# Attention on one core: a half product that waits for its partner by a semaphore of TensorE's own, and another order of the products of one step

## The chip, the cores and the metric

The kernel runs on one core of a Trainium2 chip. The metric is the device time of the whole program in microseconds (us): the median of 3 runs, beside one further execution that the hardware profiler recorded.

## The reference

Two transformer layers with shared weights, on 2048 rows of 640 numbers in float32. Each layer normalises its rows, runs an attention block with 32 heads of 20 numbers, adds the result to the rows, normalises again and runs a dense block with a squared ReLU. The part that matters here is the attention:

```python
scores = jnp.einsum("bhqd,bhkd->bhqk", q, k) * (Dh ** -0.5)
p = _softmax(scores, axis=-1)
o = jnp.einsum("bhqk,bhkd->bhqd", p, v)
```

The softmax needs the largest score of every query, so the kernel computes the scores twice: once with the queries on the partitions, to take the maximum along a row, and once with the keys on the partitions, with the maximum already subtracted, for the exponential.

## The kernel before

Heads are taken in groups of four and queries in blocks of 512: 8 groups by 4 blocks are 32 blocks of work (`NBLK`) in a layer. In a block the 2048 keys are passed in 16 steps of 128 (`NKT`). Per layer there are thus 512 steps. A head has 20 numbers, kept three times for a product in split precision, so a product contracts 60 (or 62, with the maximum) rows. Two such products fit TensorE's 128 rows side by side: `par` 0 uses rows 0 to 63, `par` 1 uses rows 64 to 127. Below they are called the lower and the upper rows.

An attention step has four kinds of work, named by letters in a hand-written order (`ORDERS`, read by `op`), which sets the order of the instructions on every engine:

- `a`, `b`: a score product (line 596), keys on the partitions, 512 queries wide, on the lower rows (`a`) or the upper ones (`b`), into one of four PSUM banks in turn. ScalarE (ACT) takes the exponential of each (line 603), which frees the bank.
- `m`, `n`: a whole product for the maxima (line 481, called from `smax`), queries on the partitions, 512 keys wide, on the lower (`m`) or upper (`n`) rows. VectorE (DVE) reduces it to a maximum (line 493), which frees the bank.
- `u`, `w`: a product for the maxima over half of the keys (256 wide, line 481, called from `smax_half`), first on the lower rows (`u`), then on the upper ones (`w`), into the two halves of one bank. One reduction on DVE (line 521) takes both.
- `V`: the exponentials times the values (line 608), eight matmul instructions on all rows, into the accumulator of the block (bank 7). It takes the exponentials of the step before.

The products for the maxima share banks 4, 5 and 6 in turn. Twelve pairs of such products are due in eight steps, whose order is `"mbubanawV" * 8`; nearly all steps of both layers use it. As the steps run ahead, the maxima belong to later blocks.

The matmuls of `u` and `w` write to one bank from two halves of the rows, so `w` is kept back until `u` is done. Before the change this goes over DVE: an empty instruction (`mark`) in DVE's queue waits for `u`, and `w` waits for that. Once a block, ACT also copies the accumulator out of PSUM (line 621).

Of the kernel before, what the change touches and what calls it, by code (L numbers as in the profile page):

```python
# [39 lines left out]
def tile_layers(  # L40
# [11 lines left out]
    nc = tc.nc  # L52
# [250 lines left out]
    def after(later, earlier, reason="one half of the rows adds to the bank that the other half has left"):  # L303
        tc.add_manual_dep(
            later.ins,
            earlier.ins.name,
            mybir.DependencyInfo(mybir.DependencyClass.Sync, mybir.DependencyReason.DATA),
            reason=reason,
        )
# [161 lines left out]
    def maxima(t):  # L471
        if t not in mx_t:
            mx_t[t] = small.tile([P, 4, 4, 6], F32, tag="mx", bufs=14, name=name("mx"))
            if t in PARTLY:
                nc.vector.memset(mx_t[t][:, :, :, :4], LEAST)
        return mx_t[t]

    def by_queries(dst, t, p, sub, c, par, keys=slice(0, QB)):

        b = 64 * par  # L480
        return nc.tensor.matmul(  # L481
            dst,
            q_t[t][b : b + 60, p, sub * P : (sub + 1) * P],
            k_t[t // NQB, c][b : b + 60, p, keys],
            start=True,
            stop=True,
        )
# [7 lines left out]
        )  # L495

    halved = {}

    def two_columns(t):

        if t not in halved:
            halved[t] = True
            nc.gpsimd.memset(maxima(t)[:, :, :, 4:], LEAST)

    def column(*x):

        halved[x] = halved.get(x, 3) + 1
        assert halved[x] < 6
        return halved[x]

    def smax_half(bank, t, p, sub, c, half, par, earlier=None):

        w = QB // 2
        dst = bank[:, par * w : (par + 1) * w]
        m = by_queries(dst, t, p, sub, c, par, slice(half * w, (half + 1) * w))
        if earlier is None:
            mark = nc.vector.nop()
            after(mark, m)
            return mark
        after(m, earlier, "matmuls on two halves of the rows write to one bank in turn")  # L520
        nc.vector.tensor_reduce(  # L521
            maxima(t)[:, p : p + 3 : 2, sub, c if not half else column(t, p, sub)],
            bank.rearrange("q (r k) -> q r k", r=2),
            axis=AX.X,
            op=ALU.max,
        )

    def step_one(t, p, sub, x, par):

        dst = ps_q("sm")  # L530
        res = xtile("rl")[:, :QB]
        by_queries(dst, t, p, sub, x, par)
        nc.scalar.activation(res, dst, AF.Relu)  # L533
        return res
# [180 lines left out]
    def qkv(first, x_src, rest, scores):  # L715
# [275 lines left out]
        15: "anbmnanbaabmbnammbnaVbmbmmbVmbananVanmbanVnambmbVanbmnaVnmbaanVmbbanmV",  # L991
        14: "mbbbanmbbmambmVanannaVmbnaaanVbmabnmVanbmbmbVnaanmbVmabmbanVbmannaVn",
        13: "baanmbVmbanambbnbmVanbmnaVnaabnmbVanbmaanVnmbbanaVmnbmabVabbmmnaVm",
        12: "mbubanawV" * 8,
    }

    def attention(first, x_src, first_rows):
# [95 lines left out]
        def op(o):  # L1093
# [17 lines left out]
            elif o == "u":  # L1111
                if parts or next_pair(parts):
                    x = parts.pop(0)
                    bank = turn.pop(0)
                    opened.append((bank, x, smax_half(banks[:, bank, :], *x, 0)))
            elif o == "w":
                if opened:
                    bank, x, mark = opened.pop()
                    smax_half(banks[:, bank, :], *x, 1, mark)
                    turn.append(bank)  # L1120
                    did(x[0])
            else:
                i = state["done"]
                if i >= last or i < last - NKT and min(st_n) < 2 * (i + 1):
                    return
                t, u = divmod(i, NKT)
                if u == 0:
                    state["acc"] = banks[:, 7, :]
                pv(state["acc"], t, u, es_of.pop(i))
                state["done"] += 1  # L1130
                if u == NKT - 1:
                    steps = finish(t, state["acc"])
                    split.update((i + j, f) for j, f in zip((4, 6, 7, 9, 11, 12), steps))
                t = rows["next"]
                if rows["at"] is not None:
                    if state["begun"] >= rows["at"]:
                        mrows_load(t)
                        rows.update(next=t + 1, at=None)
                elif t in over and t in q_t and state["begun"] >= (t - 2) * NKT + 2:
                    mrows_max(t)  # L1140
                    mrows(t)
                    rows["at"] = state["begun"] + 2
# [417 lines left out]
```

## Time and profile before

| what | value |
|---|---|
| median of 3 runs | 3538.99 us (3538.1 to 3539.18) |
| profiled execution | 3538.19 us |
| its span, first to last instruction | 3536.2 us |
| granted TensorE clock in it | 1.000 of full speed |
| busy share of PE, DVE, ACT | 100%, 77%, 75% |
| reductions of two halves (line 521), that is steps with a `u` and a `w` | 982 |

PE is TensorE's matmuls, PEld its weight loads, which run beside matmuls. A matmul of this kernel is one weight load and one matmul instruction, and a wait in front of it shows at the weight load. The ends of matmuls are modelled in the profile, and a PE that is busy 100% of the time isn't one at its peak: what holds a step up is read from starts, and from the idle time in brackets with the instruction that ended it.

### The profile page before, as it was taken

How to read it: one execution, taken by the hardware profiler on the slowest of the kernel's cores; microseconds unless marked ns; L12 is line 12 of the kernel's file. 1: busy time of each engine (PE TensorE's matmuls, PEld its weight loads, DVE VectorE, ACT ScalarE, POOL GpSimd, SP SyncE). 2: the span in 40 equal slices, each digit the busy share in tenths (PEclk: the TensorE clock that was granted, in tenths of full speed). 3: DMA queues.
4: the chain of work that ended last, by engine and by line, in shares of the span. 5: the costliest groups of instructions: out<-in, count | busy, mean ns of one | idle time of the engine just before them, and what ended most of it. 6: DMA issues, size and time to landing. Idle time of an engine off the chain costs nothing.

```text
span 3536.2 us, 70757 instructions
## 1 busy us (share of the span) xinstructions
PE 3521.2 (100%) x26542; PEld 2264.2 (64%) x26542; DVE 2731.2 (77%) x5023; ACT 2652.9 (75%) x5208; POOL 809.5 (23%) x927
## 2 busy tenths in 40 slices
PE   9999999999999999999999999999999999999999
PEld 7897444444444446999988964444444444479998
DVE  8878999999999993456567789999999999824443
ACT  3778999999999995122237789999999999932221
POOL 6531444221221111111153201221211211211110
PEclk9999999999999999999999999999999999999999
DMA  9776555323211136734477652232232111376231
GB/s 304 274 233 175 172 156 157 109 70 82 57 48 49 46 110 209 249 106 111 135 269 249 197 150 76 65 82 61 67 82 59 46 48 43 115 226 238 75 82 38
DMA packets 377413, 452.78 MB, mean 128 GB/s; under 512 B 176642, under 2 KB 223746, under 8 KB 377070
## 3 DMA queue, kind: packets, MB, share of 16 engines
q1 hardware_dynamic: 376254, 445.89, 41.6%
q8 instruction: 209, 3.42, 0.4%
q10 hardware_dynamic: 816, 2.36, 0.2%
q14 instruction: 134, 1.10, 0.1%
HBM read 273.83 MB, written 174.30 MB: 127 GB/s over the span
## 4 chain that ended last, share of the span: by engine, by line
PE 95%; DVE 2%; ACT 1%; DMA 1%; issue 1%; POOL 0%; SPq 0%; DVEq 0%; ACTq 0%
PE banks L608 29%; PE banks L481 22%; PE banks L293 13%; PE banks L596 11%; PE banks L1326 10%; PE banks L331 9%; DVE mx L493 1%; ACT e L603 1%; PE banks L1158 0%; DMA q<-d_qk 0%; ACT e L1165 0%; DVE bst L244 0%; DVE xnT L257 0%; DVE x L252 0%; DMA d_qk<-ev 0%
## 5 line engine op out<-in xcount | busy, mean ns | idle before, releaser
L603 ACT ACTIVATE e<-banks 128x512 f32<-128x512 f32 x3968 | 2034.7, 613 | 10.3 <-PE banks L596 2.2
L493 DVE TENSOR_REDUCE mx<-banks 128x1 f32<-128x512 f32 x2094 | 1346.5, 686 | 187.2 <-PE banks L596 126.6
L481 PE MATMUL banks<-k,q 60*128 60x512 f32 x4568 | 1347.7, 374 | 3.0 <-DVE v L377 1.7
L481 PEld LDWEIGHTS banks<-k,q 60*128 60x128 f32 x4568 | 763.8, 184 | 848.5 <-DVE mx L493 824.8
L596 PE MATMUL banks<-q,k 62*128 62x512 f32 x3968 | 1132.1, 432 | 0.4 <-DVE mx L541 0.4
L608 PE MATMUL banks<-e,vg 128*32 128x512 f32 x8192 | 1091.0, 605 | 1.5 <-ACT e L1165 1.5
L596 PEld LDWEIGHTS banks<-q,k 62*128 62x128 f32 x3968 | 654.5, 184 | 99.8 <-ACT e L603 36.6
L521 DVE TENSOR_REDUCE mx<-banks 128x2 f32<-128x512 f32 x982 | 670.5, 683 | 0.0
L541 DVE CUSTOM_DVE_ANT_0 rl<-banks,rl 128x512 f32<-128x512 f32 x510 | 332.8, 689 | 101.1 <-PE banks L481 91.0
L1311 ACT ACTIVATE r<-banks,b_t 128x512 f32<-128x512 f32 x96 | 66.2, 689 | 420.1 <-PE banks L293 396.3
L331 PE MATMUL banks<-xnT,wqk 64*128 64x512 f32 x2400 | 378.8, 394 | 0.3 <-ACT mark_t L333 0.3
L533 ACT ACTIVATE rl<-banks 128x512 f32<-128x512 f32 x510 | 270.8, 597 | 98.2 <-PE banks L481 89.3
L1326 PE MATMUL banks<-w,h 128*128 128x320 f32 x2304 | 340.4, 309 | 0.0
L1326 PEld LDWEIGHTS banks<-w,h 128*128 128x128 f32 x2304 | 339.2, 188 | 1.2
L293 PE MATMUL banks<-xnT,w 128*128 128x512 f32 x1440 | 329.4, 389 | 0.0
L331 PEld LDWEIGHTS banks<-xnT,wqk 64*128 64x128 f32 x2400 | 286.1, 185 | 34.2 <-issue 2.4
L293 PEld LDWEIGHTS banks<-xnT,w 128*128 128x128 f32 x1440 | 269.6, 188 | 55.3
L608 PEld LDWEIGHTS banks<-e,vg 128*32 128x32 f32 x8192 | 161.1, 108 | 165.5 <-issue 78.4
L652 POOL TENSOR_TENSOR few<-few,minus_t 128x16 f32<-128x16 f32 x62 | 179.8, 2900 | 357.9 <-DMA few<-d_s 352.5
L271 POOL CAST mr<-nt 128x32 fp32r<-128x32 f32 x64 | 13.4, 209 | 963.7 <-DVE nt L567 963.7
L331 PE MATMUL banks<-wv,xnT 64*128 64x320 f32 x1920 | 199.4, 307 | 0.9 <-ACT mark_t L333 0.9
L331 PEld LDWEIGHTS banks<-wv,xnT 64*128 64x128 f32 x1920 | 187.3, 185 | 2.5 <-ACT mark_t L333 1.4
(89 smaller groups left out, 2094.2 us busy)
## 6 DMA issues: line engine op xcount, KB each, us to landing
q<-d_qk SPq DMA_DIRECT2D x242, 240.0 KB
d_qk<-ev SPq DMA_DIRECT2D x80, 512.0 KB
k<-d_qk SPq DMA_DIRECT2D x152, 240.0 KB
x<-d_x SPq DMA_DIRECT2D x84, 320.0 KB
d_qk<-ev SPq DMA_DIRECT2D x80, 256.0 KB
d_o<-ot SPq DMA_DIRECT2D x248, 80.0 KB
ot<-d_o SPq DMA_DIRECT2D x38, 512.0 KB
d_v<-v SPq DMA_DIRECT2D x32, 512.0 KB
```

The lines of the kernel that those rows point to most:

```text
L293: nc.tensor.matmul(dst, a, b, start=(n == 0), stop=(n == last))
L331: m = nc.tensor.matmul(ch["dst"][:, :width], *pair, start=first, stop=last)
L481: return nc.tensor.matmul(dst, q_t[t][b : b + 60, p, sub * P : (sub + 1) * P], k_t[t // NQB, c][b : b + 60, p, keys], start=True, stop=True,)
L493: nc.vector.tensor_reduce(maxima(t)[:, 2 * par + p, sub, c : c + 1], dst, axis=AX.X, op=ALU.max)
L521: nc.vector.tensor_reduce(maxima(t)[:, p : p + 3 : 2, sub, c if not half else column(t, p, sub)], bank.rearrange("q (r k) -> q r k", r=2), ...
L533: nc.scalar.activation(res, dst, AF.Relu)
L541: nc.vector.tensor_tensor_reduce(out=r, in0=dst, in1=r, scale=1.0, scalar=LEAST, op0=ALU.add, op1=ALU.max, accum_out=maxima(t)[:, 2 * par ...
L596: nc.tensor.matmul(dst, k_t[t // NQB, kt // 4][b : b + 62, p, (kt % 4) * P : (kt % 4 + 1) * P], q_t[t][b : b + 62, p, :], start=True, stop ...
L603: nc.scalar.activation(es[p][:, par, :], dst, AF.Exp, scale=SCALE)
L608: nc.tensor.matmul(acc[32 * h : 32 * h + 32, :], v_t[t // NQB, kt // 8][:, kt % 8, 32 * h : 32 * h + 32], es[p][:, par, :], start=(kt == 0 ...
L652: nc.gpsimd.tensor_tensor(few, few, minus_t, op=ALU.pow)
L1326: nc.tensor.matmul(dst[:, :HALF], hs[f][:, hx, i * P : (i + 1) * P], w_2.piece(at_2(f0 + f, hw, hf)), start=(f == 0 and (hx, hw) == THREE[0]),
```

## The change

The first half product `u` now increments a semaphore of its own, `first_half`, and the second half product `w` waits for that on TensorE, without DVE. The empty instruction on DVE is gone. The order of a step is `b u b m a w n a V` in place of `m b u b a n a w V`.

```diff
+    first_half = tc.alloc_semaphore("first_half")
+    firsts_done = [0]
...
         m = by_queries(dst, t, p, sub, c, par, slice(half * w, (half + 1) * w))
         if earlier is None:
-            mark = nc.vector.nop()
-            after(mark, m)
-            return mark
-        after(m, earlier, "matmuls on two halves of the rows write to one bank in turn")
-        nc.vector.tensor_reduce(
+            firsts_done[0] += 1
+            m.then_inc(first_half, 1)
+            tc.no_tile_sem_insts.add(m.ins.name)
+            tc.add_to_no_dep_group(f"first half {firsts_done[0]}", m.ins)
+            return m, firsts_done[0]
+        m_1, n = earlier
+        m.wait_op(first_half, n, "sem-ge")
+        tc.declare_no_dep(m.ins, m_1.ins, reason="waits for the semaphore of the first half")
+        tc.declare_fence(m.ins, group=f"first half {n}")
+        r = nc.vector.tensor_reduce(
             maxima(t)[:, p : p + 3 : 2, sub, c if not half else column(t, p, sub)],
...
+        tc.declare_no_dep(r.ins, m_1.ins, reason="waits for the second half, which waits for the first")
...
-        12: "mbubanawV" * 8,
+        12: "bubmawnaV" * 8,
```

`first_half` is counted up, one for each `u`, and `w` waits until the count has reached the number of its own `u`. `u` no longer increments the semaphore that the scheduler keeps for TensorE.

## The prediction

> **What bounds the kernel now.** I read the page first: its length, the chain that ended last, the costliest groups.
>
> ```profile
> span 3536.2 us, 70757 instructions
> PE 95%; DVE 2%; ACT 1%; DMA 1%; issue 1%; POOL 0%; SPq 0%; DVEq 0%; ACTq 0%
> L603 ACT ACTIVATE e<-banks 128x512 f32<-128x512 f32 x3968 | 2034.7, 613 | 10.3 <-PE banks L596 2.2
> ...
> L521 DVE TENSOR_REDUCE mx<-banks 128x2 f32<-128x512 f32 x982 | 670.5, 683 | 0.0
> ...
> L621 ACT COPY o<-banks 128x512 f32<-128x512 f32 x62 | 38.2, 617 | 0.0
> ```
>
> The 982 reductions count the steps with a `u` and a `w`, so a step's gain or loss counts 982 times at most. The chain says PE, but ACT's 3968 exponentials fill 2034.7 us with hardly an idle moment: in the attention two engines are close together. So next the timeline of one step (start, length, engine, line; the last number counts instructions), then of ACT alone in the same stretch.
>
> ```profile
> 901.55 0.49 PE L481 MATMUL banks<-k,q 60*128 60x512 f32 x1
> 901.55 0.49 PE L596 MATMUL banks<-q,k 62*128 62x512 f32 x1
> 901.88 0.28 PE L481 MATMUL banks<-k,q 60*128 60x256 f32 x1
> 901.89 0.51 PE L596 MATMUL banks<-q,k 62*128 62x512 f32 x2
> 902.08 1.29 DVE L493 TENSOR_REDUCE mx<-banks 128x1 f32<-128x512 f32 x2 [0.16 <-PE banks L596]
> 902.12 0.40 PE L481 MATMUL banks<-k,q 60*128 60x512 f32 x1
> 902.24 0.44 PE L596 MATMUL banks<-q,k 62*128 62x512 f32 x1
> 902.27 0.18 PEld L481 LDWEIGHTS banks<-k,q 60*128 60x128 f32 x1
> 902.36 0.30 PE L481 MATMUL banks<-k,q 60*128 60x256 f32 x1
> 902.60 1.06 PE L608 MATMUL banks<-e,vg 128*32 128x512 f32 x8
> 903.28 0.68 DVE L521 TENSOR_REDUCE mx<-banks 128x2 f32<-128x512 f32 x1
> ...
> 904.02 0.18 PEld L481 LDWEIGHTS banks<-k,q 60*128 60x128 f32 x1
> 904.23 0.18 PEld L596 LDWEIGHTS banks<-q,k 62*128 62x128 f32 x1
> 904.66 1.06 PE L608 MATMUL banks<-e,vg 128*32 128x512 f32 x8
> 905.66 0.50 PE L481 MATMUL banks<-k,q 60*128 60x512 f32 x1
> ```
>
> ```profile
> 902.11 0.60 ACT L603 ACTIVATE e<-banks 128x512 f32<-128x512 f32 x1
> 902.61 0.59 ACT L603 ACTIVATE e<-banks 128x512 f32<-128x512 f32 x1
> 903.09 0.60 ACT L603 ACTIVATE e<-banks 128x512 f32<-128x512 f32 x1
> 903.56 0.62 ACT L603 ACTIVATE e<-banks 128x512 f32<-128x512 f32 x1
> ```
>
> Call the first product's start (901.55) R. The rows are, in the order of the program, m and b at R, u (901.88), b again (901.89, with the a behind it in one row), n (902.12), the last a (902.24), w (902.36), V (902.60). The next but one step begins at 905.66, so two steps take 4.11, one 2.055. That number is a loop through ACT: b to its exponential 0.56 (902.11), four exponentials to the end of the fourth (903.56 + 0.62 = 904.18), 0.05 to the weight load of the next step's last a, which takes over that bank (904.23), 0.43 to V (904.66), 1.00 of V to the next R (905.66). Sum 4.11. PE alone would do a little better, as a step shows in which the bank is free early:
>
> ```profile
> 910.87 1.06 PE L608 MATMUL banks<-e,vg 128*32 128x512 f32 x8
> 912.84 0.18 PEld L596 LDWEIGHTS banks<-q,k 62*128 62x128 f32 x1 [0.30 <-ACT e L603]
> 913.26 1.06 PE L608 MATMUL banks<-e,vg 128*32 128x512 f32 x8
> ...
> 914.79 0.18 PEld L596 LDWEIGHTS banks<-q,k 62*128 62x128 f32 x1
> ...
> 915.29 0.64 PE L608 MATMUL banks<-e,vg 128*32 128x512 f32 x4
> ```
>
> From 913.26 to 915.29 is 2.03, with that weight load 0.50 ahead of V. The step before it, 2.39, is one of 62 in which the copy of an accumulator holds ACT up. So: PE needs 2.03, the ACT loop 2.055, and a third loop through DVE is shorter: m's reduction at R + 0.53 (902.08), the third 1.20 later, its end at 903.96, n's weight load at 904.02, with room left before n starts.
>
> **The change, part by part.** *The empty DVE instruction goes, 982 times.* `w`'s weights load at 902.27 and it starts at 902.36, 0.24 after n (902.12) on the same rows; b to n, both 512 wide, is 0.23. So w waits for its rows, not for the mark, and the removal gains 0. What hides the wait is the place of w behind n. In the new order n stands behind w, and that cover is gone.
>
> *The order.* Both rows keep their columns (three of 512, one of 256), so PE's sum is the same if m may start behind u while the second b, which stands ahead of it, still waits for its rows. The last steps of a layer have no maxima left and run b, b, a, a, V, which is this case:
>
> ```profile
> 1334.37 0.29 PEld L596 LDWEIGHTS banks<-q,k 62*128 62x128 f32 x2 [0.84 <-ACT e L603]
> 1334.37 0.63 PE L596 MATMUL banks<-q,k 62*128 62x512 f32 x2
> 1334.37 0.73 PE L596 MATMUL banks<-q,k 62*128 62x512 f32 x3
> 1334.91 0.60 ACT L603 ACTIVATE e<-banks 128x512 f32<-128x512 f32 x1
> ```
>
> The PE rows are what runs by 1334.60 and by 1334.85. The second product began at 1334.51 (its end, 1334.37 + 0.63 = 1335.00, less the 0.49 to 0.50 of a first product), 0.14 behind the first: too soon for the upper rows, which a first product holds 0.33 (901.55 to 901.88). It is an a, started ahead of the second b, whose weights were loading by 1334.49. So starts pass each other: u at R, m at R + 0.22 (0.33 less half a product, 0.12), the a's at R + 0.45 and R + 0.69 as now. Cost 0. (The Trainium skill, page "TensorE: Matmul & The Clock Gate", Part 3, The mechanism, has matmuls strictly in order in start and in end; the rows above disagree on the start. By that rule the time would be that of rival B.)
>
> *Who tells of a product's end, and when.* Ends do keep the order. In the projection of the values two streams alternate on the two halves of the rows, and the program's order matched to the starts gives this (the PE rows are what runs at 306.60, 306.65 and 306.75):
>
> ```profile
> 306.33 0.54 PE L331 MATMUL banks<-wv,xnT 64*128 64x320 f32 x3
> 306.42 0.45 PE L331 MATMUL banks<-wv,xnT 64*128 64x320 f32 x2
> 306.57 0.30 PE L331 MATMUL banks<-wv,xnT 64*128 64x320 f32 x1
> 306.78 0.43 ACT L377 COPY v<-banks 128x320 f32<-128x320 f32 x1 [0.58 <-PE banks L331]
> ```
>
> The product that started at 306.33 closes a chain and is over by 306.65, yet the copy that waits for it starts at 306.78: 0.05 after the end (306.42 + 0.31) of a product on the other rows that stands just ahead of it in the program and that nobody waits for. A signal is given only when everything ahead in the program is done. And a second signal follows the first late: m and b end together (901.55 + 0.49 = 902.04), m's reduction starts 0.04 later, b's exponential 0.07 later; where b is alone (1334.37 + 0.50) its exponential follows after 0.04.
>
> Three things follow for `b u b m a w n a V`:
> - u (256 wide, beside the first b) is computed early, but its signal comes behind b's: b's end R + 0.49, plus 0.07 for a second signal, is R + 0.56. Until then w's weight load waits at the head of TensorE's queue, and the loads of n, of the last a and V are queued behind it. Weights to product 0.09 (902.27 to 902.36): w at R + 0.65 in place of R + 0.57. n, 0.12 later, at R + 0.77. From a last product of 512 to V 0.34 (904.66 less 904.23, less 0.09): V at R + 1.11. With V's 1.00 a step takes 2.11. The wait for an own signal isn't in this trace; its bounds are 0.04 behind b's end (a lone signal) and 0.10 (0.03 more for each of two signals ahead): steps of 2.08 and 2.14. I take 0.07, the row of a second signal.
> - m's reduction waits for the second b, which stands ahead of m: its start R + 0.34, 0.40 long, plus 0.07: R + 0.81, now R + 0.53. The DVE loop becomes 0.81 + 1.20 + 0.68 to the end of the third reduction, which is now n's and frees n's own bank, + 0.06 to its weight load, + 0.43 to V, + 1.00 = 4.18 for two steps, 2.09 each. Under 2.11, but it would hold the step if u's signal came sooner.
> - b comes first and its exponential gains 0.03: the ACT loop falls to 4.08, 2.04 each, and no longer decides.
>
> *Else moved.* The loads issued on SP's queue hang on the first score product of a step, which stays in its place but for m; the fetch of a later block's queries and Pool's fill of its spare columns now hang on u in place of m, one product apart, and no loop above runs through them. 0.
>
> *The sum.* Ordinary steps: 982 less 62 is 920, at 2.11 less 2.055: +51 us. The 62 steps behind a copy (2.39): ACT's free time in a step grows by 0.05, so the copy's delay is partly taken up there, 0.05 to 0.1 each: -6 us. Together +45 on the profiled execution's 3538.19, that is 3583; its time lies 0.8 under the median, which I count as nothing. With the bounds of u's signal: 920 times 0.025 and 0.085, less the same 6: 3555 to 3610.
>
> **The rivals.**
> - A, faster: signals do not wait for their turn across the two halves of the rows. u's signal is there by R + 0.45, before w's weights are needed at R + 0.48; m's reduction starts at R + 0.65. Then the ACT loop's 2.04 is the longest: 920 times -0.015 is -14, 3524. It decides if u's signal comes before R + 0.48. Against it stands the 0.15 between a chain's end and its copy above; for it, that this was seen on products of 64 rows and another stage.
> - B, slower still: m may not start ahead of the second b here. Then m at R + 0.34, the a's at R + 0.57 and R + 0.81, V at R + 1.15, a step of 2.15: +87, less 6, 3619. The b, b, a, a steps speak against it.
> - C, no change: u's signal comes just after b's, 0.01 rather than 0.03 later, and TensorE reads its own signal faster than ACT does, so w's weights load by R + 0.50; and the reductions catch up in the steps behind a copy. A step stays within 0.01 of 2.055: 3538. The 0.07 of b's exponential speaks against it.
>
> (The same section of the Trainium skill has 26 ns per signal, one behind another, and ends in program order; here the trace agrees, 0.03 for the second.)
>
> **How the numbers follow.** 0.73 for the forecast, 0.10 for A, 0.08 for B, 0.09 for C. The time is the forecast's, 3583, its own range 3555 to 3610. The range for 8 in 10 leaves out A and C, 0.19, and reaches up past B: 3545 to 3625. A change of 0.2%, 7 us, is about what a measurement here can tell. Faster 0.10 (A), same 0.09 (C), slower 0.81 (the forecast and B).
>
> **What would show it.** Right: V to V 2.11 in ordinary steps; w's weight load 0.56 after the first b, behind an idle time; m's reduction 0.8 after it, though m starts at 0.22; the first exponential 0.03 sooner; n's and the last a's weights loading right behind w's start. Wrong: w's weight load by R + 0.48 (A); m starting behind the second b (B); V to V of 2.055 with the last a's weights still 0.05 behind an exponential's end (C). If DVE's loop turned out to hold the step, w's load would be early and n's late.

## The result and the profile after

The changed kernel takes 3593.23 us (median of 4 runs with the profiled one, 3592.2 to 3597.2) against 3538.55 us before on the same chips: 1.0157 times as long, 95% interval 1.0140 to 1.0175. Forecast were 3583 and a range of 3545 to 3625. The profiled execution took 3593.89 us, 55.7 more than that of before.

The page of the changed kernel: span, the exponentials, the reductions of two halves (the lines of the code have moved by 7 or 8: 596 is now 604, 603 is 611, 608 is 616, 521 is 528).

```profile
span 3592.0 us, 69772 instructions
L611 ACT ACTIVATE e<-banks 128x512 f32<-128x512 f32 x3968 | 2046.4, 613 | 54.1 <-PE banks L604 3.3
L528 DVE TENSOR_REDUCE mx<-banks 128x2 f32<-128x512 f32 x984 | 671.5, 682 | 1.8 <-PE banks L481 1.8
```

ACT's idle time in front of the exponentials has grown from 10.3 to 54.1 us: ACT is no longer what a step waits for. (Two steps more than before have a `u` and a `w`, 984; the account below takes 982.) The timeline of one step of the changed kernel says what a step waits for now (the row at 902.65 is from the view of a shorter stretch, in which the product m stands alone, the row at 902.95 from one of ACT alone):

```profile
901.43 1.07 PE L616 MATMUL banks<-e,vg 128*32 128x512 f32 x8
...
902.42 0.49 PE L604 MATMUL banks<-q,k 62*128 62x512 f32 x1
...
902.43 0.62 PE L481 MATMUL banks<-k,q 60*128 60x256 f32 x2
...
902.76 0.52 PE L604 MATMUL banks<-q,k 62*128 62x512 f32 x2
...
903.01 0.18 PEld L481 LDWEIGHTS banks<-k,q 60*128 60x128 f32 x1 [0.17 <-PE banks L481]
903.01 0.39 PE L481 MATMUL banks<-k,q 60*128 60x256 f32 x1
903.05 0.18 PEld L604 LDWEIGHTS banks<-q,k 62*128 62x128 f32 x1
...
903.12 0.19 PEld L481 LDWEIGHTS banks<-k,q 60*128 60x128 f32 x1
903.12 0.42 PE L604 MATMUL banks<-q,k 62*128 62x512 f32 x1
903.22 0.69 DVE L493 TENSOR_REDUCE mx<-banks 128x1 f32<-128x512 f32 x1 [0.23 <-PE banks L604]
903.24 0.38 PE L481 MATMUL banks<-k,q 60*128 60x512 f32 x1
...
903.55 1.07 PE L616 MATMUL banks<-e,vg 128*32 128x512 f32 x8
...
905.67 1.06 PE L616 MATMUL banks<-e,vg 128*32 128x512 f32 x8
```

```profile
902.65 0.39 PE L481 MATMUL banks<-k,q 60*128 60x512 f32 x1
```

```profile
902.95 0.60 ACT L611 ACTIVATE e<-banks 128x512 f32<-128x512 f32 x1
```

R is 902.42, the first b. The step from V to V is 2.12 (901.43 to 903.55, 903.55 to 905.67). w's weights load at 903.01, R + 0.59, after 0.17 idle ended by a product of line 481, its own u: that is 0.09 to 0.10 behind the end of b (902.42 + 0.49 = 902.91; these rows are rounded to 0.01). The next weights on those rows, n's, follow 0.11 later (903.12). n starts at 903.24, V 0.31 later. m, at 902.65, did start ahead of the second b (902.76), but its reduction starts only at 903.22, R + 0.80, and the profile names a product of line 604, the second b, as what ended the wait. The first exponential is at R + 0.53, 0.03 sooner than before.

The profile infers who ended a wait, but the trace also records when each semaphore is counted up, and that shows the delay of the signals directly. `first_half` is counted up by u alone. In this step u starts at 902.43, its record ends at 902.81 (modelled), and the count comes only at 902.97, after that of the first b (902.93). m needs the same look, because there is another explanation for its late reduction: all products but u count up one semaphore of the scheduler's, so a wait for m could be a wait for a number to which the second b adds. But that semaphore isn't counted up at all between 902.93 and 903.17, where the second b ends (902.76 + 0.39 = 903.15), though m's record ends at 902.65 + 0.39 = 903.04. m's signal itself is late.

In the steps behind a copy of the accumulator some comes back:

```profile
1029.31 1.07 PE L616 MATMUL banks<-e,vg 128*32 128x512 f32 x8
...
1031.58 0.64 PE L616 MATMUL banks<-e,vg 128*32 128x512 f32 x4
```

2.27 in place of 2.39. The account: 920 ordinary steps at 2.12 in place of 2.055 are +60 us, 62 steps behind a copy at -0.12 are -7, together +53 of the 55.7 measured; the rest is within the rounding of these rows.

### The profile page after: what moved, and what is told of

Same layout as the page of the kernel before. It is cut to its first block, busy times and chain, and to the rows that moved or that the text cites. A ratio compares the mean times of both kernels' runs of the same rounds, so it can differ in the third digit from the quotient of the medians.

```text
span 3592.0 us, 69772 instructions
## 1 busy us (share of the span) xinstructions
PE 3576.8 (100%) x26544; PEld 2155.6 (60%) x26544; DVE 2727.6 (76%) x5023; ACT 2664.6 (74%) x5208; POOL 809.2 (23%) x927
## 4 chain that ended last, share of the span: by engine, by line
PE 97%; DVE 1%; ACT 1%; DMA 1%; issue 1%; POOL 0%; SPq 0%; DVEq 0%; ACTq 0%
PE banks L616 28%; PE banks L604 19%; PE banks L481 16%; PE banks L293 13%; PE banks L331 10%; PE banks L1334 9%; PE banks L1166 0%; ACT e L1173 0%; DVE bst L244 0%; DVE mx L493 0%; ACT e L611 0%; DVE x L252 0%; DVE xnT L257 0%; DMA q<-d_qk 0%; DMA d_qk<-ev 0%
## 5 line engine op out<-in xcount | busy, mean ns | idle before, releaser
L611 ACT ACTIVATE e<-banks 128x512 f32<-128x512 f32 x3968 | 2046.4, 613 | 54.1 <-PE banks L604 3.3
L493 DVE TENSOR_REDUCE mx<-banks 128x1 f32<-128x512 f32 x2092 | 1427.6, 686 | 247.5 <-PE banks L604 219.7
L481 PE MATMUL banks<-k,q 60*128 60x256 f32 (+1 forms) x4570 | 1417.0, 390 | 2.2 <-DVE v L377 1.3
L604 PEld LDWEIGHTS banks<-q,k 62*128 62x128 f32 x3968 | 596.7, 184 | 836.0 <-ACT e L611 829.5
L481 PEld LDWEIGHTS banks<-k,q 60*128 60x128 f32 x4570 | 694.8, 184 | 185.3 <-PE banks L481 157.8
```

The lines of the kernel that those rows point to most:

```text
L481: return nc.tensor.matmul(dst, q_t[t][b : b + 60, p, sub * P : (sub + 1) * P], k_t[t // NQB, c][b : b + 60, p, keys], start=True, stop=True,)
L493: nc.vector.tensor_reduce(maxima(t)[:, 2 * par + p, sub, c : c + 1], dst, axis=AX.X, op=ALU.max)
L604: nc.tensor.matmul(dst, k_t[t // NQB, kt // 4][b : b + 62, p, (kt % 4) * P : (kt % 4 + 1) * P], q_t[t][b : b + 62, p, :], start=True, stop ...
L611: nc.scalar.activation(es[p][:, par, :], dst, AF.Exp, scale=SCALE)
```

## The experiments

In all of them "theory S" is that of the prediction: a product's signal is given only when everything ahead of it in the program is done. In the changed kernel it bears on two products, u behind the first b and m behind the second. Rival W puts the loss on the wait for an own semaphore as such, rival P on the packing of the two halves of the rows.

**The two parts of the change apart.** The semaphore with the old order:

```diff
-        12: "bubmawnaV" * 8,
+        12: "mbubanawV" * 8,
```

> The semaphore alone, in the old order of a step (m b u b a n a w V). Theory S (a product's signal is given only behind everything ahead of it in the program, and in the new order u stands behind a b twice as wide): here m and b, ahead of u, end at 0.49 behind the step's start, u itself at 0.61, so w's weights could load by 0.66 to 0.70 and are wanted at 0.70. Steps stay at 2.055, 3533 to 3545 us. Rival W (TensorE waiting for a semaphore of its own is dear in itself): the wait costs here as it does in the changed kernel, steps of 2.10 or more, 3570 us or more. Rival P (the new order packs the two halves of the rows worse): no change here either, 3538 us.

Measured: 3537.28 us, ratio to before 0.9995, interval 0.9986 to 1.0005. W falls as far as this order goes: the same wait on the same semaphore costs nothing here, where w stands behind n.

```profile
901.54 0.49 PE L481 MATMUL banks<-k,q 60*128 60x512 f32 x1
...
902.21 0.18 PEld L481 LDWEIGHTS banks<-k,q 60*128 60x128 f32 x1
...
902.35 0.28 PE L481 MATMUL banks<-k,q 60*128 60x256 f32 x1
902.56 0.64 PE L616 MATMUL banks<-e,vg 128*32 128x512 f32 x4
```

w's weights load 0.67 behind the step's start, w starts 0.81 behind it, as before, and V is at 1.02, in a step that is one of the shortest.

The new order with the empty DVE instruction (the kernel before, with one line changed):

```diff
-        12: "mbubanawV" * 8,
+        12: "bubmawnaV" * 8,
```

> The new order alone (b u b m a w n a V), w kept back by the empty DVE instruction as before. Theory S: u's signal reaches DVE 0.07 behind b's end, at 0.56 of the step, and TensorE 0.07 later, at 0.63 in place of the 0.58 of the changed kernel; steps of 2.17, 3630 to 3645 us, slower than the changed kernel. Rival W: with no semaphore of TensorE's own the loss is gone, 3540 us or less. Rival P: as the changed kernel, 3593 us.

Measured: 3653.04 us, 1.0321 (1.0304 to 1.0338), slower than the changed kernel and 8 us above the expectation. The order brings the whole loss, and the semaphore takes about half of it back. W falls, as the loss is there without a semaphore of TensorE's own. P alone doesn't explain the 60 us between this kernel and the changed one, which pack alike; the next run decides on it.

```profile
899.62 1.06 PE L608 MATMUL banks<-e,vg 128*32 128x512 f32 x8
...
900.62 0.49 PE L596 MATMUL banks<-q,k 62*128 62x512 f32 x1
...
901.26 0.18 PEld L481 LDWEIGHTS banks<-k,q 60*128 60x128 f32 x1 [0.23 <-DVEq L517]
...
901.81 1.06 PE L608 MATMUL banks<-e,vg 128*32 128x512 f32 x8
```

w's weights load 0.64 behind the first b, where 0.63 was expected, on the mark (line 517). V follows 0.55 later, and V to V is 2.19, 0.02 more than expected.

**u ahead of the first b.** Two neighbours of the changed kernel's order are exchanged; on the chip they start together anyway.

```diff
-        12: "bubmawnaV" * 8,
+        12: "ubbmawnaV" * 8,
```

> The changed kernel with u ahead of the first b (u b b m a w n a V). Theory S: u's signal now waits for nothing, w's weights load by 0.47 and w starts behind the second b without a wait. m still stands behind the second b, so its reduction still starts at 0.80, and the loop through DVE takes over: 0.80 + 1.20 + 0.68 + 0.05 to n's weights, 0.43 to V, 0.99 to the next step, 4.15 for two steps, 2.08 each; with less loss at the 62 copies 3540 to 3555 us. If only u's signal mattered (no loop through DVE): 2.04 a step, 3515 to 3528 us. Rivals W and P: as the changed kernel, 3593 us.

Measured: 3559.28 us, 1.0056 (1.0041 to 1.0071), 34 us less than the changed kernel and 4 above the expectation. This is the cleanest test of S: the products and their waits are the same, only the place of u in the program differs. W and P, which expected 3593, are out. The semaphore shows the cause: over the 984 u's of a run, `first_half` is counted up 0.54 behind u's start (median) in the changed kernel and in the two runs below that keep u behind the first b, and 0.39 to 0.40 behind it here and in the two runs below with u first. What is left of the loss is the other half:

```profile
900.12 0.38 PE L481 MATMUL banks<-k,q 60*128 60x256 f32 x1
...
900.69 0.53 PE L481 MATMUL banks<-k,q 60*128 60x256 f32 x2
...
900.92 0.69 DVE L493 TENSOR_REDUCE mx<-banks 128x1 f32<-128x512 f32 x1 [0.26 <-PE banks L604]
901.15 1.07 PE L616 MATMUL banks<-e,vg 128*32 128x512 f32 x8
...
902.12 1.51 DVE L493 TENSOR_REDUCE mx<-banks 128x1 f32<-128x512 f32 x2
...
903.30 1.06 PE L616 MATMUL banks<-e,vg 128*32 128x512 f32 x8
```

```profile
902.86 0.18 PEld L481 LDWEIGHTS banks<-k,q 60*128 60x128 f32 x1
```

```profile
905.32 0.64 PE L616 MATMUL banks<-e,vg 128*32 128x512 f32 x4
```

w now starts 0.57 behind the step's start (900.69), without a wait. m's reduction is still at 0.80, released by line 604. The third reduction starts at 902.12 (its row holds the next one too), is over 0.68 later, and n's weights load 0.06 behind that (902.86): the loop through DVE. Two steps take 4.17 (901.15 to 905.32), 2.08 each, as worked out in the prediction's second point.

**m ahead of the second b, u still behind the first.** The other half alone:

```diff
-        12: "bubmawnaV" * 8,
+        12: "bumbawnaV" * 8,
```

> The changed kernel with m ahead of the second b (b u m b a w n a V): the other half of the two shifts alone. m's reduction starts at 0.65 in place of 0.80, u stays behind the first b. Theory S: w's weights still load at 0.58, steps stay at 2.12 to 2.13, 3585 to 3597 us. If the late reduction of m were the loss: 2.04 to 2.06, 3520 to 3540 us.

Measured: 3593.6 us, 1.0155 (1.0141 to 1.0169), the time of the changed kernel.

```profile
900.25 1.06 PE L616 MATMUL banks<-e,vg 128*32 128x512 f32 x8
...
901.25 0.49 PE L604 MATMUL banks<-q,k 62*128 62x512 f32 x1
...
901.83 0.18 PEld L481 LDWEIGHTS banks<-k,q 60*128 60x128 f32 x1 [0.17 <-PE banks L481]
...
901.90 0.69 DVE L493 TENSOR_REDUCE mx<-banks 128x1 f32<-128x512 f32 x1 [0.23 <-PE banks L481]
...
902.38 1.06 PE L616 MATMUL banks<-e,vg 128*32 128x512 f32 x8
```

m's reduction starts at 0.65 and is now released by line 481, its own product. w's weights still load at 0.58, and a step is still 2.13. So in the changed kernel u's signal sets the time; m's lies just under it and shows only when u's is gone.

**w at its old place behind n**, with both products still behind a b:

```diff
-        12: "bubmawnaV" * 8,
+        12: "bubmanawV" * 8,
```

> The changed kernel with w at its old place behind n (b u b m a n a w V). u still stands behind the first b, but its signal at 0.58 is in time there. m still stands behind the second b. Theory S: the wait of w is hidden and the loss stays, now through DVE alone: m's reduction at 0.80, the third at 2.01, its end 2.69, the weights of n, whose bank it frees, at 2.74, then n and w to V 0.54, V 0.99: 4.28 for two steps, 2.14 each, 3600 to 3622 us. If the wait of w for u were the whole loss: 2.04 to 2.055, 3520 to 3540 us.

Measured: 3601.34 us, 1.0178 (1.0164 to 1.0191).

```profile
899.71 1.07 PE L616 MATMUL banks<-e,vg 128*32 128x512 f32 x8
900.69 0.68 DVE L528 TENSOR_REDUCE mx<-banks 128x2 f32<-128x512 f32 x1
...
901.43 0.18 PEld L481 LDWEIGHTS banks<-k,q 60*128 60x128 f32 x1 [0.30 <-DVE mx L528]
...
901.97 1.06 PE L616 MATMUL banks<-e,vg 128*32 128x512 f32 x8
...
903.99 0.64 PE L616 MATMUL banks<-e,vg 128*32 128x512 f32 x4
```

Hiding w's wait without moving m doesn't help: the third reduction is over at 901.37, n's weights wait for it until 901.43, and two steps take 4.28, 2.14 each, the number expected.

**Both ahead.** u first, m ahead of the second b:

```diff
-        12: "bubmawnaV" * 8,
+        12: "ubmbawnaV" * 8,
```

> The changed kernel with u first and m ahead of the second b (u b m b a w n a V). Theory S: neither u nor m waits for a signal ahead of it, m's reduction starts at 0.65, and the first b's exponential comes 0.03 sooner than in the old order. The loop through DVE falls to 2.01 a step, the one through ACT to 2.04, TensorE alone takes 2.03: steps of 2.04 in place of 2.055, and ACT's slack takes up part of the 62 copies: 3512 to 3526 us, faster than both kernels. Rival W: 3570 us or more, as w still waits for TensorE's own semaphore. Rival P: 3538 us or more.

> The same order once more (u b m b a w n a V, w waiting for the semaphore of u), to narrow its interval. Theory S and the run before: steps of 2.04, 3521 to 3526 us, 0.995 to 0.996 of the kernel before. If that run's gain was chance: 3533 us or more.

Measured: 3523.07 us, 0.9955 (0.9940 to 0.9969), and in the second run 3524.44 us, 0.9958 (0.9946 to 0.9970): faster than both kernels, though w still waits for TensorE's own semaphore, for which W expected 3570 or more. A step of the second run, and its first exponential:

```profile
901.70 0.49 PE L604 MATMUL banks<-q,k 62*128 62x512 f32 x1
...
902.35 0.69 DVE L493 TENSOR_REDUCE mx<-banks 128x1 f32<-128x512 f32 x1 [0.16 <-PE banks L481]
```

```profile
902.23 1.08 ACT L611 ACTIVATE e<-banks 128x512 f32<-128x512 f32 x2
```

m's reduction is at 0.65, and b's exponential 0.53 behind b, not 0.56 as before the change.

**Only b ahead of m**, the rest as in the old order, to see where that gain is from:

```diff
-        12: "bubmawnaV" * 8,
+        12: "bmubanawV" * 8,
```

> The semaphore with the old order but for one exchange: b ahead of m at the start of a step (b m u b a n a w V). Theory S: b's signal no longer follows that of m, so the first exponential starts 0.53 behind the step's start in place of 0.56; m's reduction starts 0.03 later, which has room. The ACT loop falls from 4.11 to 4.08 for two steps: 2.04 a step, 3520 to 3527 us. If the delay of b's exponential had another cause than m's signal ahead of it: as with the semaphore alone, 3537 us.

Measured: 3522.72 us, 0.9955 (0.9942 to 0.9969).

```profile
901.40 0.50 PE L604 MATMUL banks<-q,k 62*128 62x512 f32 x1
```

```profile
901.94 0.60 ACT L611 ACTIVATE e<-banks 128x512 f32<-128x512 f32 x1
```

0.54 from b to its exponential, 0.02 to 0.03 less than with the semaphore and the old order, and 14.6 us less of the program's time (3537.28 less 3522.72). Over the whole trace two steps in a row take 4.07 (median), 4.11 with the old order: the 0.03 that the expectation took from the ACT loop. The exponential of b was late because m's signal stood ahead of it. That bears out the ACT loop as what bounded the kernel before.

## Why the prediction was right, point by point

- *ACT's loop bounds the kernel before.* Right: taking 0.03 from it gains 15 us, although m's reduction starts 0.03 later by the same exchange; taking the mark away gains nothing.
- *The empty DVE instruction costs nothing.* Right in the time (0.9995). The reason was a little off: I read from w's start that it waits for its rows and not for the mark. The mark did hold PE a little: before the change 3 of 929 ordinary steps (V to V of 1.95 to 2.25) were shorter than the 2.03 that the prediction took for PE alone; with the semaphore in the old order 395 of 927 are, most of them 2.00 to 2.02. Two steps in a row take 4.11 (median) in both: the next step gives the time back, and the ACT loop hid the mark's cost.
- *m may start ahead of the second b.* Right, 902.65 against 902.76. Rival B is out; so, between the two halves of the rows, is the rule of strict order in start that the Trainium skill has in "TensorE: Matmul & The Clock Gate", Part 3, The mechanism. Its other half, order in end, holds here for the signals, and this case turns on it; in the records, whose ends are modelled, m is over at 903.04 and the second b at 903.15. The 26 ns per signal that the prediction names stand in the same Part 3 of the Trainium skill under "The cost: per-tile semaphore tail"; the 0.03 by which b's exponential came sooner when b was put ahead of m agrees.
- *u's signal comes behind b's.* Right, and shown by the exchange of u and b alone. Three sizes were off: w's weights load 0.09 to 0.10 behind b's end, not 0.07, and so near the upper of the prediction's two bounds (0.10); w holds up n's weights for 0.11, where the sum had 0.09; from n to V it is 0.31, not 0.34. Two were too small and one too large, so that the step came to 2.12 against 2.11 by luck in part; over 920 steps that is 9 of the 11 us missed in the sum of the profiled execution (+45 forecast, +55.7 measured).
- *The loop through DVE at 2.09.* 2.08, once u's signal no longer covers it.
- *The copies.* 0.12 each in place of 0.05 to 0.1, the right way.
- *Rivals A and C* are out: w's weights load at 0.59, and a step isn't 2.055.

## What to carry to other kernels

Two products on different halves of TensorE's rows started in either order here, but whoever waited for one of them also waited for everything ahead of it in the program, on the other half too. So put a product that somebody waits for ahead of one on the other rows that ends later or together with it, if its waiter is on the longest loop. Here that exchange was worth 34 us for u and the first b, which start within 0.01 us of each other, another 36 for m and the second b (3559 to 3523) once u was first, and nothing (3593.6) while u still held the step, and 15 for the first b and m. When a wait is moved to a faster path, look at what its old place hid: the mark was covered by n, and the new order took n away.

## What the runs showed of the hardware

Weight loads passed each other here as products do: the last a's weights (903.05) were loaded ahead of those of n (903.12), which stands ahead of it in the program. A wait of TensorE for its own product, 0.09 to 0.10 behind the end of the product whose signal goes first, was shorter than the way through DVE in the same order, where the weights load at 0.64 in place of 0.59, 0.15 behind that end.
